# Transposing two units' activations by DMA instead of on TensorE, with half-width tiles at the start of a layer

## The chip, the cores and the metric

One core of one Trainium2 chip. The metric is the time of one execution in device microseconds; below, "time" is the median of the fast runs. Profiles come from the hardware profiler, one execution each. TensorE is PE, VectorE DVE, ScalarE ACT, GpSimd POOL, SyncE SP. SP and POOL issue the DMAs (and ACT the last store). The granted clock is TensorE's, as a share of its full speed.

## The reference, cut to what matters

Chunked attention is followed by a two-layer feed-forward block:

```python
scores = scale * q_c @ k_c.T             # 8 batches x 8 heads, chunks of 64 tokens, head size 64
attn   = exp(scores) / sum               # in each chunk
x      = (attn @ v_c) as (4608 tokens, 512)
h      = x @ w_in                        # 512 -> 2048
g      = h * 1 / (1 + exp(-beta * h))
out    = g @ w_out                       # 2048 -> 512
```

## The kernel before

The 4608 tokens are 18 units of 256; two units form a block of 512 (units 4 and 5 are block 2). The attention of later units is woven between the matmuls of earlier blocks. A unit has two halves `s` of 128 tokens. For each half, `emit_norm` (DVE) divides the weighted sum by its denominator and gives x in fp16. It has to be transposed before the first layer, on PE or by DMA:

```python
def emit_xt_pe(u, s, copy=nc.scalar.copy):
    xf = x16_t.pop((u, s)).rearrange("p r h d -> p (r h d)")
    ...                                                     # a PSUM bank for xp
    for g in range(4):
        nc.tensor.transpose(out=xp[:, g, :], in_=xf[:, g * 128:(g + 1) * 128], identity=ident)
    copy(out=xt_at(u, s), in_=xp)                           # on ACT

def emit_xt_dma(u, s):
    xf = x16_t.pop((u, s)).rearrange("p r h d -> p (r h d)")
    nc.sync.dma_start_transpose(out=xt_at(u, s), in_=xf)    # on SP's queue
```

Before the change, units 0 to 5 go by PE and units 6 to 17 by DMA. One first-layer tile, and where its result goes:

```python
def emit_m(j, m, c0=0, n=None, later=False):    # tile m of block j; n columns from c0, all 512 by default
    hps = ps_p.tile([128, 512], FP32, tag="p", name="hps")   # one of four PSUM banks, shared with ops
    for kk in range(4):
        nc.tensor.matmul(out=hps[:, 0:n], lhsT=w_in..., rhs=xt..., ...)
    sg = ...                                                 # ACT: tanh(beta/2 * hps)
    ...                                                      # DVE: gt = (sg + 1) * hps; then the bank is free
```

`emit_t(j, t, k0, k1)` are the second layer's matmuls of output tile t (`ops`), `emit_sc`/`emit_pv` a unit's scores and weighted sum, `emit_T` transposes q and k. `loads_to(u)` puts a unit's loads of q, k and v (six for unit 9) on POOL's DMA queue. They convert fp32 to fp16 and write 128-byte rows.

The softmax here doesn't subtract the row's maximum and nothing guards it: scores larger than these inputs give would overflow.

Of the kernel before, what the change touches and what calls it, by code (L numbers as in the profile page):

```python
# [15 lines left out]
def kernel(  # L16
# [16 lines left out]
    KFF = DFF // 128  # L33
# [91 lines left out]
    def loads_to(u):  # L125
        while nxt[0] <= min(u, NU - 1):
            load_unit(nxt[0])
            nxt[0] += 1
# [16 lines left out]
    def emit_T(u, which=("kT", "qT")):  # L145
        for nm in which:
            src, dst = {"kT": (k_t, kT), "qT": (q_t, qT)}[nm]
            a = src.pop(u)
            t = qt_p.tile([128, H, CH, 2], FP16, tag=nm, name=nm)
            dst[u] = t  # L150
            if u >= XU:
                nc.sync.dma_start_transpose(
                    out=t.rearrange("p h s e -> p (h s e)").rearrange("p (j t) -> p j t", t=128),
                    in_=a.rearrange("p h r d -> p (h r d)"),
                )
                continue
            nc.vector.transpose(
                out=t.rearrange("p h s e -> p (h s e)").bitcast(FP32).rearrange(
                    "p (h i r) -> p h r i", h=H, r=2),
                in_=a.rearrange("p h r d -> p (h r d)").bitcast(FP32).rearrange(  # L160
                    "p (h r i) -> p h r i", h=H, r=2),
            )
        if which[-1] == "qT" and u not in (6, 7, 8):
            loads_to(u + 4)

    def emit_gate(u):
        nc.gpsimd.tensor_copy(out=gate, in_=x16_t[u, 1][:, 0, 0, 0:1])
# [86 lines left out]
    def emit_pv(u, where=("x", "s")):  # L254
        et = et_t.pop(u)
        for s in (1, 0) if u >= MU else (0, 1):
            i = 2 * u + s
            if where[s] == "p":
                x = [ps_p.tile([128, 4, 128], FP32, tag="p", name=f"y{r}") for r in range(2)]
            else:  # L260
                pool = {"x": ps_x, "s": ps_s}[where[s]]
                x = [pool.tile([128, 2, 4, 128], FP32, tag=where[s], name="x")]
            for g in range(4):
                for r in range(2):
                    for c in range(2):
                        nc.tensor.matmul(  # L266
                            out=(x[0][64 * c:64 * c + 64, r, g, 0:D + 1] if len(x) == 1 else
                                 x[r][64 * c:64 * c + 64, g, 0:D + 1]),
                            lhsT=(et[64 * r:64 * r + 64, s, 4 * c + g, :] if u < XU else
                                  et[64 * r:64 * r + 64, g % 2, 4 * s + 2 * c + g // 2, :]),  # L270
                            rhs=vbig[64 * r:64 * r + 64, i, 4 * c + g, 0:D + 1],
                        )
            x_t[u, s] = x
# [6 lines left out]
    def emit_norm(u, s):  # L280
        x = x_t.pop((u, s))
        rd = rd_p.tile([128, 2, 4, 1], FP32, tag="rd", name="rd")
        x16 = x_p.tile([128, 2, 4, D], FP16, tag="x16", name="x16")
        for r, z in [(slice(0, 2), x[0])] if len(x) == 1 else list(enumerate(x)):
            nc.vector.reciprocal(out=rd[:, r], in_=z[..., D:D + 1])  # L285
            o = x16[:, r]
            nc.vector.tensor_tensor(  # L287
                out=o, in0=z[..., 0:D], in1=rd[:, r].to_broadcast(list(o.shape)), op=ALU.mult
            )
        x16_t[u, s] = x16  # L290

    def xt_at(u, s):
        j, o = unit_block[u]
        if j not in xt_t:
            xt_t[j] = xt_p.tile([128, 4, 4, 128], FP16, tag="xt", name="xt")
        return xt_t[j][:, 2 * o + s]

    def emit_xt_pe(u, s, copy=nc.scalar.copy):
        xf = x16_t.pop((u, s)).rearrange("p r h d -> p (r h d)")
        tag = "s" if u < 2 and (u, s) != (1, 0) else "xp"[s]  # L300
        xp = {"x": ps_x, "s": ps_s, "p": ps_p}[tag].tile([128, 4, 128], FP16, tag=tag, name="xp")
        for g in range(4):
            nc.tensor.transpose(out=xp[:, g, :], in_=xf[:, g * 128:(g + 1) * 128], identity=ident)  # L303
        copy(out=xt_at(u, s), in_=xp)  # L304
# [11 lines left out]
    def emit_xt_dma(u, s):  # L316
        xf = x16_t.pop((u, s)).rearrange("p r h d -> p (r h d)")
        nc.sync.dma_start_transpose(out=xt_at(u, s), in_=xf)
# [3 lines left out]
    def emit_m(j, m, c0=0, n=None, later=False):  # L322
        n = blocks[j][1] * UNIT if n is None else n
        if j not in gt_t:
            gt_t[j] = gt_p.tile([128, KFF, 512], FP16, tag="gt", name="gt")
        hps = ps_p.tile([128, 512], FP32, tag="p", name="hps")
        xr = xt_t[j].rearrange("p t (r k) (c q) -> p (t r) (k c) q", r=2, c=2)
        for kk in range(KDM):
            nc.tensor.matmul(  # L329
                out=hps[:, 0:n],  # L330
                lhsT=w_in16[m // 2][:, kk, (m % 2) * 128:(m % 2) * 128 + 128],
                rhs=xr[:, c0 // CH:(c0 + n) // CH, 2 * (kk % 2) + kk // 2, :],
                start=(kk == 0),
                stop=(kk == KDM - 1),
            )
        sg = sg_p.tile([128, 512], FP32, tag="sg", name="sg")

        def act():
            nc.scalar.activation(  # L339
                out=sg[:, 0:n], in_=hps[:, 0:n], func=ACTF.Tanh, scale=beta2[:, m:m + 1])  # L340

        def vec():
            nc.vector.scalar_tensor_tensor(  # L343
                out=gt_t[j][:, m, c0:c0 + n], in0=sg[:, 0:n], scalar=1.0, in1=hps[:, 0:n],
                op0=ALU.add, op1=ALU.mult,
            )

        if later:
            return act, vec
        act()  # L350
        vec()
# [3 lines left out]
    def emit_t(j, t, k0=0, k1=None):  # L355
        k1 = KFF if k1 is None else k1
        if k0 == 0:
            ops_t[j, t] = ps_p.tile([128, DM], FP32, tag="p", name="ops")
        ops = ops_t[j, t]
        for kk in range(k0, k1):  # L360
            nc.tensor.matmul(  # L361
                out=ops,
                lhsT=gt_t[j][:, kk, t * 128:(t + 1) * 128],
                rhs=w_out16[kk // 4][:, kk % 4, :],
                start=(kk == 0),
                stop=(kk == KFF - 1),
            )
        if k1 < KFF:
            return
        osb = osb_p.tile([128, DM], FP32, tag="osb", name="osb")  # L370
        nc.scalar.activation(out=osb, in_=ops, func=ACTF.Copy, scale=0.5)  # L371
        r0 = blocks[j][0] * UNIT + t * 128
        nc.sync.dma_start(out=out[r0:r0 + 128, :], in_=osb)
# [20 lines left out]
    with tc.manual_schedule():  # L394
# [111 lines left out]
                emit_ex(4)  # L506
        emit_t(1, 0, 0, 8)
        emit_pv(4)
        emit_norm(4, 0)
        emit_norm(4, 1)  # L510
        emit_T(5)
        emit_T(6)
        emit_t(1, 0, 8)
        emit_xt_pe(4, 0)
        emit_xt_pe(4, 1)
        emit_t(1, 1, 0, 8)
        emit_sc(5)
        emit_t(1, 1, 8)
        emit_pv(5)
        emit_norm(5, 0)  # L520
        emit_norm(5, 1)
        emit_T(7)
        emit_t(1, 2, 0, 8)
        emit_xt_pe(5, 0)
        emit_xt_pe(5, 1)
        emit_sc(6)
        emit_t(1, 2, 8)
        for m in range(KFF):
            emit_m(2, m)
            if m == 0:  # L530
                emit_pv(6)
                emit_norm(6, 0)
                emit_xt_dma(6, 0)
            if m == 1:
                emit_norm(6, 1)
                emit_gate(6)
                emit_xt_dma(6, 1)
                loads_to(10)
                emit_t(1, 3, 0, 8)
                emit_T(8)  # L540
            if m == 4:
                emit_sc(7)
            if m == 5:
                emit_t(1, 3, 8)
            if m == 7:
                emit_pv(7)
                emit_norm(7, 0)
                emit_xt_dma(7, 0)
            if m == 8:
                emit_norm(7, 1)  # L550
                emit_gate(7)
                emit_xt_dma(7, 1)
                loads_to(11)
# [90 lines left out]
```

## Time and profile before

| | |
|---|---|
| time, 3 runs | 288.05 us (287.95 to 288.5) |
| profiled span, granted PE clock | 286.6 us, 0.999 |
| PE busy | 280.4 us |
| PE waits on a DMA | none |

The prediction shows the page's main lines, and lines of the timeline (start in us, duration, instruction, count). This is PE's timeline where block 3 starts (start in us, duration, instruction, count), then the view of the last transpose of x that this block needs, issued at 91.24 us:

```profile
94.71 1.89 PE L361 MATMUL ops<-wout,gt 128*128 128x512 f16 x8
96.44 0.81 PE L329 MATMUL hps<-xt,win 128*128 128x512 f16 x3
```
```profile
DMA to landing us min/median/max: 4.1/4.1/4.1
```

The transpose lands at 95.3 us and PE wants it at 96.44: 1.1 us to spare, which no list of waits shows. At block 5 it is 1.3 us (154.24 against 155.54).

### The profile page before, as it was taken

What the parts mean: (1) busy time and instruction counts of PE and PEld (TensorE: products, weight loads), DVE (VectorE), ACT (ScalarE), POOL (GpSimd) and SP (SyncE); (2) the same over time, 40 slices, a digit from 0 to 9 for tenths busy, and PEclk for the clock granted to TensorE, in tenths of its full rate; (3) what the DMA queues carried; (4) which work ended last, traced back from release to release, by engine and by line L of the source; (5) the groups of instructions that cost most, each with busy time, mean ns of one, the idle gap of its engine ahead of it and who ended that gap; (6) DMA issues with size and microseconds to landing.
All of it is one profiled execution on the core that took longest, in us unless ns stands there. A gap on an engine that the chain in (4) does not pass through costs nothing.

```text
span 286.6 us, 6655 instructions
## 1 busy us (share of the span) xinstructions
PE 280.4 (98%) x2777; PEld 136.4 (48%) x2777; DVE 141.9 (49%) x260; ACT 147.0 (51%) x225; POOL 95.7 (33%) x125
## 2 busy tenths in 40 slices
PE   6989999999999999999999999999999999999995
PEld 3564456545544444444444444444444444444444
DVE  2778444776567544534454445454554545333300
ACT  3478228774557545454545454554545444444411
POOL 8853678487172992070907160000000000000000
PEclk9999999999999999999999999999999999999999
DMA  8999999999999999999999999565451212010012
GB/s 193 175 196 206 182 180 215 206 166 165 153 95 182 155 176 167 165 119 168 137 158 145 143 124 171 129 75 128 57 129 39 73 39 73 37 39 37 37 73 75
DMA packets 139997, 37.14 MB, mean 130 GB/s; under 512 B 126912, under 2 KB 135488, under 8 KB 139968
## 3 DMA queue, kind: packets, MB, share of 16 engines
q0 software_dynamic: 99136, 17.83, 82.4%
q1 hardware_dynamic: 40688, 18.83, 32.2%
q8 instruction: 22, 0.36, 0.5%
q14 instruction: 7, 0.06, 0.1%
q10 hardware_dynamic: 144, 0.07, 0.1%
HBM read 36.71 MB, written 9.44 MB: 161 GB/s over the span
## 4 chain that ended last, share of the span: by engine, by line
PE 96%; ACT 1%; POOL 1%; issue 1%; DVE 0%; DVEq 0%; POOLq 0%
PE hps L329 44%; PE ops L361 43%; PE warm L381 2%; PE x L266 2%; PE sc L238 1%; PE sc L225 1%; PE ops L600 1%; ACT xt L304 1%; PE xp L303 1%; POOL h L401 1%; PE sc L198 1%; POOL vbig L113 1%; ACT et L208 0%; PE y L266 0%; PE xp L311 0%
## 5 line engine op out<-in xcount | busy, mean ns | idle before, releaser
L343 DVE SCALAR_TENSOR_TENSOR gt<-sg,hps 128x512 f16<-128x512 f32 (+1 forms) x153 | 99.1, 654 | 107.4 <-ACT sg L339 107.2
L339 ACT ACTIVATE sg<-hps,beta 128x512 f32<-128x512 f32 (+1 forms) x153 | 100.4, 663 | 72.9 <-PE hps L329 72.8
L329 PE MATMUL hps<-xt,win 128*128 128x512 f16 (+1 forms) x612 | 136.8, 367 | 0.8 <-ACT xt L304 0.7
L361 PE MATMUL ops<-wout,gt 128*128 128x512 f16 x560 | 131.2, 379 | 0.0
L329 PEld LDWEIGHTS <-win 128*128 128x128 f16 x612 | 58.1, 98 | 62.1 <-issue 1.0
L361 PEld LDWEIGHTS <-gt 128*128 128x128 f16 x560 | 53.9, 98 | 63.4
L371 ACT ACTIVATE osb<-ops 128x512 f32<-128x512 f32 x35 | 20.9, 598 | 42.5 <-PE ops L361 42.5
L113 POOL DMA_DIRECT2D vbig<-in_v_dram x40 | 34.1, 871 | 9.6 <-DMA wout<-in_moe_w_out_dram 3.7
L99 POOL DMA_DIRECT2D qu<-in_q_dram x22 | 18.7, 863 | 40.1 <-DMA qT<-qu 37.1
L287 DVE TENSOR_TENSOR x<-x,rd 128x512 f16<-128x512 f32 x31 | 21.4, 691 | 1.2
L99 POOL DMA_DIRECT2D ku<-in_k_dram x22 | 18.9, 877 | 0.6 <-DMA ku<-in_k_dram 0.6
L285 DVE RECIPROCAL rd<-x 128x8 f32<-128x8 f32 x31 | 6.2, 200 | 12.0 <-PE x L266 12.0
L247 ACT ACTIVATE et<-sc 128x1024 f16<-128x1024 f32 (+1 forms) x8 | 6.4, 811 | 8.2 <-PE sc L238 8.2
L231 ACT ACTIVATE et<-sc 128x1024 f16<-128x1024 f32 x10 | 10.2, 1018 | 0.2
L266 PEld LDWEIGHTS <-et 64*64 64x64 f16 x576 | 6.0, 107 | 7.3 <-issue 3.8
L381 PE MATMUL warm<-idle 128*128 128x512 f16 x22 | 8.2, 518 | 0.0
L105 POOL DMA_DIRECT2D ku<-in_k_dram x9 | 6.8, 756 | 2.5 <-DMA win<-in_moe_w_in_dram 1.3
L266 PE MATMUL x<-vbig,et 64*64 64x65 f16 x496 | 7.3, 194 | 0.2 <-ACT et L208 0.2
L105 POOL DMA_DIRECT2D qu<-in_q_dram x9 | 6.8, 767 | 1.4 <-DMA win<-in_moe_w_in_dram 0.7
L612 DVE TENSOR_SCALAR osb<-ops 128x256 f32<-128x256 f32 (+1 forms) x2 | 0.7, 357 | 12.1 <-PE ops L600 12.1
L131 POOL DMA_DIRECT2D win<-in_moe_w_in_dram x8 | 6.0, 757 | 1.2 <-DMA vbig<-in_v_dram 0.9
L304 ACT COPY xt<-xp 128x512 f16<-128x512 f16 x9 | 5.1, 588 | 2.3 <-PE xp L303 2.2
(46 smaller groups left out, 73.4 us busy)
## 6 DMA issues: line engine op xcount, KB each, us to landing
out_dram<-osb SPq DMA_DIRECT2D x35, 256.0 KB, 3.7
vbig<-in_v_dram POOLq DMA_DIRECT2D x32, 128.0 KB, 7.6
qu<-in_q_dram POOLq DMA_DIRECT2D x20, 128.0 KB, 4.9
ku<-in_k_dram POOLq DMA_DIRECT2D x20, 128.0 KB, 6.8
win<-in_moe_w_in_dram POOLq DMA_DIRECT2D x8, 256.0 KB, 9.0
wout<-in_moe_w_out_dram POOLq DMA_DIRECT2D x4, 512.0 KB, 12.3
qu<-in_q_dram POOLq DMA_DIRECT2D x3, 256.0 KB, 7.7
ku<-in_k_dram POOLq DMA_DIRECT2D x3, 256.0 KB, 8.0
```

The costliest lines, as they stand in the source:

```text
L99: nc.gpsimd.dma_start(out=tv[off:off + n, sp], in_=src[b, :, s:s + n, :].rearrange("h p d -> p h d"),)
L105: nc.gpsimd.dma_start(out=t[off // 2:(off + n) // 2], in_=src[b, :, s:s + n, :].rearrange("h (p r) d -> p h r d", r=2),)
L113: nc.gpsimd.dma_start(out=vbig[off:off + n, i, :, 0:D], in_=v[b, :, s:s + n, :].rearrange("h p d -> p h d"),)
L231: nc.scalar.activation(out=et, in_=sc, func=ACTF.Exp, scale=scale)
L266: nc.tensor.matmul(out=(x[0][64 * c:64 * c + 64, r, g, 0:D + 1] if len(x) == 1 else x[r][64 * c:64 * c + 64, g, 0:D + 1]), lhsT=(et[64 * r ...
L287: nc.vector.tensor_tensor(out=o, in0=z[..., 0:D], in1=rd[:, r].to_broadcast(list(o.shape)), op=ALU.mult)
L329: nc.tensor.matmul(out=hps[:, 0:n], lhsT=w_in16[m // 2][:, kk, (m % 2) * 128:(m % 2) * 128 + 128], rhs=xr[:, c0 // CH:(c0 + n) // CH, 2 * ...
L339: nc.scalar.activation(out=sg[:, 0:n], in_=hps[:, 0:n], func=ACTF.Tanh, scale=beta2[:, m:m + 1])
L343: nc.vector.scalar_tensor_tensor(out=gt_t[j][:, m, c0:c0 + n], in0=sg[:, 0:n], scalar=1.0, in1=hps[:, 0:n], op0=ALU.add, op1=ALU.mult,)
L361: nc.tensor.matmul(out=ops, lhsT=gt_t[j][:, kk, t * 128:(t + 1) * 128], rhs=w_out16[kk // 4][:, kk % 4, :], start=(kk == 0), stop=(kk == K ...
L371: nc.scalar.activation(out=osb, in_=ops, func=ACTF.Copy, scale=0.5)
L381: nc.tensor.matmul(out=d[:, 0:w], lhsT=idle[:, 0:128], rhs=idle[:, 0:w])
```

## The change

The intent: take 16 transposes off the engine that sets the time, and hide the DMA's latency by starting block 2's first layer with tiles that need unit 4 only.

```diff
         emit_pv(4)
+        emit_norm(4, 1)
+        emit_xt_dma(4, 1)
+        emit_T(5)
         emit_norm(4, 0)
-        emit_norm(4, 1)
-        emit_T(5)
+        emit_xt_dma(4, 0)
         emit_T(6)
         emit_t(1, 0, 8)
-        emit_xt_pe(4, 0)
-        emit_xt_pe(4, 1)
...
         emit_norm(5, 0)
+        emit_xt_dma(5, 0)
         emit_norm(5, 1)
+        emit_xt_dma(5, 1)
         emit_T(7)
         emit_t(1, 2, 0, 8)
-        emit_xt_pe(5, 0)
-        emit_xt_pe(5, 1)
         emit_sc(6)
         emit_t(1, 2, 8)
-        for m in range(KFF):
-            emit_m(2, m)
+        order = [(m, 0, 256) for m in range(6)]
+        for m in range(6, KFF):
+            order.append((m, 0, None))
+            if m < 12:
+                order.append((m - 6, 256, 256))
+        done = 0
+        for m, c0, n in order:
+            emit_m(2, m, c0, n)
+            done += 1 if n else 2
...      # the other work hangs on the same places: unit 6 after half tiles 1 and 3, emit_sc(7) after the first full
...      # tile, emit_t(1, 3, 8) after half (0, 256), emit_pv(7) and emit_norm(7, ..) after halves (2, 256), (3, 256)
```

More of the change, by code (lines that the diff above doesn't have):

```diff
@@ L520 @@
         emit_norm(5, 0)
+        emit_xt_dma(5, 0)
         emit_norm(5, 1)
+        emit_xt_dma(5, 1)
         emit_T(7)
         emit_t(1, 2, 0, 8)
-        emit_xt_pe(5, 0)
-        emit_xt_pe(5, 1)
         emit_sc(6)
         emit_t(1, 2, 8)
-        for m in range(KFF):
-            emit_m(2, m)
-            if m == 0:
+        order = [(m, 0, 256) for m in range(6)]
[7 more added lines that the diff above has]
+            done += 1 if n else 2
+            if done == 2:
                 emit_pv(6)
@@ L533 @@
                 emit_xt_dma(6, 0)
-            if m == 1:
+            if done == 4:
                 emit_norm(6, 1)
@@ L540 @@
                 emit_T(8)
-            if m == 4:
+            if (m, n) == (6, None):
                 emit_sc(7)
-            if m == 5:
+            if (m, c0, n) == (0, 256, 256):
                 emit_t(1, 3, 8)
-            if m == 7:
+            if (m, c0, n) == (2, 256, 256):
                 emit_pv(7)
@@ L548 @@
                 emit_xt_dma(7, 0)
-            if m == 8:
+            if (m, c0, n) == (3, 256, 256):
                 emit_norm(7, 1)
```

## The prediction

> **What bounds the kernel now.** I read the page's first two parts, then the chain of work that ended last, the chain between 62 and 76 us (where the four transposes of x stand), and the busy time by stretch.
>
> ```profile
> span 286.6 us, 6655 instructions
> PE 280.4 (98%) x2777; PEld 136.4 (48%) x2777; DVE 141.9 (49%) x260; ACT 147.0 (51%) x225; POOL 95.7 (33%) x125
> ...
> PE 96%; ACT 1%; POOL 1%; issue 1%; DVE 0%; DVEq 0%; POOLq 0%
> ```
> ```profile
> 66.12 0.45 PE xp L303 x8
> 66.57 1.73 PE ops L361 x8
> 68.30 0.64 PE sc L238 x64
> 68.94 1.83 PE ops L361 x8
> 70.77 0.38 PE x L266 x32
> 71.14 1.83 PE ops L361 x8
> 72.98 0.45 PE xp L303 x8
> 73.42 0.64 PE sc L238 x64
> ```
> ```profile
> 62.00:76.00 14.00, 14.00 (x259) 7.36 (x258) 7.72 (x16) 6.43 (x11) 9.24 (x11) 1.00 2.11 168
> 76.00:96.00 20.00, 20.00 (x214) 9.30 (x213) 13.45 (x24) 13.04 (x19) 9.83 (x14) 1.00 1.34 140
> 96.00:260.00 164.00, 164.00 (x1359) 75.55 (x1358) 77.35 (x136) 83.58 (x122) 35.60 (x43) 1.00 1.03 113
> ```
>
> The page says that TensorE is busy for 98% of the span and carries 96% of the chain. The chain lines show eight `xp` transposes of unit 4 in 0.45 us and eight of unit 5 in another 0.45 us, in the middle of a stream without a hole. The stretches (columns: us, then busy us of PE, PEld, DVE, ACT and POOL, then granted clock, DMA share, GB/s) show PE without a gap from 62 to 260 us at full clock. So the time is the sum of what TensorE is given: an instruction taken from it shortens the run by its own spacing, unless TensorE then waits for something.
>
> **What the Trainium skill says.** "TensorE: Matmul & The Clock Gate", section "Back-to-back issue gap", gives N/2.4 + 2.5 ns between isolated warm matmuls of N columns, and for sustained streams 81 ns at N=128 and 131 ns at N=512. This trace follows the first formula: eight 512-column matmuls take 1.73 us (216 ns each), eight 128-column transposes 0.45 us (56 ns each). I use these. The same page, "Part 4: PE-mode transpose", puts a transpose at about 275 ns in a kernel. The instruction table here has a duration of 219 ns, but that is latency: the spacing of 56 ns is what the stream pays, so counting 16 durations would overstate the gain fourfold. "DMA: Bandwidth & Descriptors", section "Issuing engines are not separate DMA queues", says that DMAs from different engines run on the same 16 DMA engines and interleave. The trace agrees: the same xt transpose landed 2.5 us after issue at 79.1 us, where the loads were quiet (DMA share 0.29 in 78 to 82), and 7.2 us after issue at 105.1 us, beside loads (share 2.27 in 102 to 108). "Perfetto Trace Analysis", section "Identifying the Most-Contended Engine", warns that matmul busy share is no measure of roofline headroom; I use it only to say that no gap is left.
>
> **The change part by part.** Removed: 16 transposes from TensorE, 0.45 + 0.45 = 0.90 us of the path by the chain's lines, 0.89 by 16 x 55.8 ns. Four ScalarE copies of about 0.59 us go too. ScalarE is busy 6.43 of the 14 us there and TensorE waited for none of them, so they weren't on the path.
>
> Added to TensorE: six tiles of four 512-column matmuls become twelve of four 256-column ones. Widths from the block before, which has both:
>
> ```profile
> 46.11 0.61 PE L329 MATMUL hps<-xt,win 128*128 128x256 f16 x4
> 46.56 1.03 PE L361 MATMUL ops<-wout,gt 128*128 128x512 f16 x4
> 47.42 0.39 PE L303 MATMUL xp<-ident,x 128*128 128x128 f16 x4
> 47.65 0.60 PE L329 MATMUL hps<-xt,win 128*128 128x256 f16 x4
> ```
>
> In the last line four start within 0.60 minus one latency of 0.27, so 0.109 us apart; a half tile is 0.437 us, a full one 0.863 (4 x 0.216). Splitting a tile costs 0.011 us, six cost 0.07. Weight loads (98 ns) still fit under 109 ns.
>
> Moved: unit 4's x now goes out by DMA. From the order of instructions, unit 4's second half is normalized first, at about 65.3 us, and its first half at about 67.4 us (after unit 5's q and k transposes). The first half-width tile needs both and comes at 75.73 - 0.89 = 74.84 us. That leaves 7.4 us for the later one, just more than the worst xt landing, 7.2 us. Unit 5's halves are issued at about 71.6 and 72.9 us, since one issue takes the queue 1.2 us. The first full tile needs them after six half tiles (2.62 us), the weighted sum of unit 6 (0.47 with its change of shape) and eight output matmuls (1.73): 4.82 us on, at 79.66 us. That is 6.8 us after the later issue; the median landing of the 24 xt transposes is 2.9 us (list of DMA issues). The six half tiles exist to buy these 4.8 us. I expect no wait on either.
>
> Added behind TensorE: VectorE. In the run of tiles at the end of this layer it is already late in the kernel before:
>
> ```profile
> 88.24 0.69 DVE L343 SCALAR_TENSOR_TENSOR gt<-sg,hps 128x512 f16<-128x512 f32 x1 [0.17 <-ACT sg L339]
> 88.85 0.20 DVE L285 RECIPROCAL rd<-x 128x8 f32<-128x8 f32 x1
> 89.08 0.69 DVE L287 TENSOR_TENSOR x<-x,rd 128x512 f16<-128x512 f32 x1
> 89.69 0.68 DVE L343 SCALAR_TENSOR_TENSOR gt<-sg,hps 128x512 f16<-128x512 f32 x1
> 90.28 0.20 DVE L285 RECIPROCAL rd<-x 128x8 f32<-128x8 f32 x1
> 90.52 0.69 DVE L287 TENSOR_TENSOR x<-x,rd 128x512 f16<-128x512 f32 x1
> ```
>
> Spacings: a full gate product 0.60 us, a normalization 0.84. The pairs of the block before (x2 groups of 1.02 us, second duration 0.41) give 0.33 us behind a half product. In before, a tile arrives each 0.86 us, so VectorE gains 0.26 us a tile. In after, a full and a half tile arrive each 1.30 us and cost 0.93, and unit 7's two normalizations (1.68 us) fall among them.
>
> Step by step from 0 at the first half tile: on TensorE tile 8 starts at 9.90, its second-half partner (tile 2) at 10.76, tile 9 at 11.67 (after unit 7's weighted sum), then 12.54, tile 10 at 12.97, 13.84, tile 11 at 14.27, 15.14, tile 12 at 15.57. ScalarE can start a full tile 1.065 us after TensorE does, and VectorE 0.72 after that, so tile 8's product starts at 11.69 and tile 2's at 12.29. Then: normalization at 12.62, tile 9 at 13.46, tile 3's half at 14.06, second normalization at 14.39, tile 10 at 15.23. This ends at 15.92. By the pool's four banks, as the built program assigns them, tile 12 is written into tile 10's bank: TensorE wants it at 15.57 and gets it at about 15.95. That is a wait of 0.38 us, the one I expect. Tile 11 (bank free at about 14.18, wanted at 14.27) just passes, and after tile 12 VectorE catches up.
>
> The scores of unit 6 wait for the second normalization of unit 5, which ends at about 72.40 us against 72.46 wanted: a few hundredths at most.
>
> Sum: -0.89 + 0.07 + 0.38 = -0.44 us, so 288.05 - 0.44 = 287.6 us.
>
> **The rivals.** First: no bank wait. If VectorE is 0.4 us earlier than I reckon, the whole -0.82 stays: 287.2 us. For it: in before, the wait list of TensorE names no VectorE wait here, although the backlog there reached four products back to back. Against: the before has no half tiles among its normalizations. Second: a DMA wait takes the transposes' place. Unit 4's later transpose is issued at about 67.4 us among loads (DMA share 2.03 in 66 to 72), and a landing after 7.4 us would stop TensorE before its first half tile. For it: 7.2 us was seen at share 2.27. Against: the store issued at 66.8 us landed in 3.7 us. Another 1 us of delay costs nearly 1 us, so 288.0 to 289.5 us. Third: ScalarE becomes the bound on the half tiles, since 0.48 us of duration exceeds TensorE's 0.437. Against: in the pairs of the block before two activations take 1.05 us against 1.30 of TensorE, and the weighted sum and eight output matmuls interrupt the six. I give it nothing.
>
> **Range and chances.** Most likely some of the bank wait (0.2 to 0.6 us), so 287.4 to 287.8. About one in five that it is absent (287.2), about one in eight that a DMA lands late (288 or more). Runs of the same kernel spread over 0.55 us (287.95 to 288.5). So 287.0 to 288.3 should hold it 8 times in 10. None of the cases reaches 2% (5.8 us): within 2% 0.985, faster 0.005, slower 0.01.
>
> **What would show it.** Right: no PE transposes after the first two blocks; unit 6's scores start about 0.9 us earlier than 73.35 us; four 256-column matmuls per 0.44 us; xt transposes of unit 4 landed before the first half tile; one PE gap of about 0.4 us late in this layer, released by VectorE's gate product. Wrong: a PE wait on an xt transpose before the first half or first full tile (late landing), a gap after it elsewhere, or no gap and a full 0.8 us gain. I'd be wrong altogether if the earlier loads and transposes upset the later DMA traffic and PE gaps appear after 96 us.

## The result, and the profile after

The changed kernel takes 289.64 us (289.53 to 290.23, 6 runs) against 288.36 us of before (287.95 to 289.33, 6 runs, which include the three above): ratio 1.0045, 95% interval 1.0027 to 1.0063. A ratio is the mean time of one kernel's fast runs over that of the other's of the same rounds, so not quite the ratio of the medians quoted.

So it is 1.3 us slower, where 0.44 us faster was foreseen. That is under half a per cent, but the interval lies above 1. From the page of the changed kernel:

```profile
span 287.8 us, 6697 instructions
PE 90%; DMA 3%; DVE 2%; ACT 1%; POOL 1%; issue 1%; DVEq 0%; POOLq 0%
```

A DMA is on the chain now, with 3% of the span. The piece of the chain that is it (start, us, what):

```profile
73.30 7.60 DMA xt<-x
80.89 0.14 issue
81.03 1.02 PE hps L329 x4
```

The last transpose of unit 5 is issued at 73.30 and lands 7.60 us later; the first full-width tile starts right behind it. PE's timeline (in brackets: idle before, and what ended it):

```profile
72.76 0.71 PE L238 MATMUL sc<-qT,kT 32*64 32x64 f16 x64
75.14 1.04 PE L329 MATMUL hps<-xt,win 128*128 128x256 f16 x8
79.10 1.04 PE L329 MATMUL hps<-xt,win 128*128 128x256 f16 x8
81.03 1.02 PE L329 MATMUL hps<-xt,win 128*128 128x512 f16 x4 [0.90 <-DMA xt<-x]
92.21 3.61 PE L329 MATMUL hps<-xt,win 128*128 128x512 f16 x16 [0.23 <-DVE gt L343]
```

Unit 6's scores start at 72.76 us, before 73.35: the gain of the removed transposes is there (0.59 us, and this run's first layer had begun 0.30 us later). The half tiles start without a wait at 75.14, so unit 4's transposes are in time. Then the two gaps. The brackets count idle from the modelled end of the matmul before. What the stream loses is the spacing of starts beyond the usual one: at 81.03 it is 1.17 - 0.11 = 1.06 us, at 92.21 it is 0.50 - 0.11 = 0.39 us.

DVE ahead of the second gap, in the order that the prediction reckoned (two products, a normalization, two products, a normalization):

```profile
88.86 0.20 DVE L285 RECIPROCAL rd<-x 128x8 f32<-128x8 f32 x1
89.09 0.69 DVE L287 TENSOR_TENSOR x<-x,rd 128x512 f16<-128x512 f32 x1
89.70 1.02 DVE L343 SCALAR_TENSOR_TENSOR gt<-sg,hps 128x512 f16<-128x512 f32 x2
90.64 0.20 DVE L285 RECIPROCAL rd<-x 128x8 f32<-128x8 f32 x1
90.87 0.69 DVE L287 TENSOR_TENSOR x<-x,rd 128x512 f16<-128x512 f32 x1
91.48 1.61 DVE L343 SCALAR_TENSOR_TENSOR gt<-sg,hps 128x512 f16<-128x512 f32 x3
```

Tile 10's product starts at 91.48 without a pause behind the normalization, and the bank is free 0.7 us later: at 92.2, when tile 12 starts.

**A measure without the start-up.** The first first-layer matmul starts anywhere from 14.80 to 16.62 us in the 14 profiles, whatever the kernel, so spans mix in noise larger than the effect. I compare the PE stream: from the start of the first first-layer matmul to the start of the last output matmul. Before: 283.45 - 15.28 = 268.17 us. After: 284.40 - 15.58 = 268.82, that is +0.65. The parts: -0.89 (transposes) + 0.07 (splits) + 1.06 + 0.39 = +0.63 us.

**Behind the last matmul** the changed kernel is slower once more: 3.41 us to the end of the span in place of 3.16. SP ends with nine waits in a row for DMA semaphores, in a fixed order and 0.06 us apart. The store that lands last (2.24 us after the last matmul starts, in both) is the last of these waits in before, while in the changed kernel four more waits follow it. I take it that the four added DMAs on SP's queue shift which semaphore tells of which store; this is read from the traces and wasn't tried by itself. All nine other profiles with both units' transposes by DMA have a tail of 3.40 or 3.41 us too; the split-only run, which keeps them on PE, has 3.16. With two DMAs added (e4 below) six waits follow the last landing, and the tail is 3.53 us. Only e10's 3.31 us has another reason: its last store lands 2.39 us after the last matmul starts, not 2.24.

### The profile page after: what moved, and what is told of

It reads as the page before. It is cut to its first block, busy times and chain, and to the rows that moved or that the text cites. A ratio compares the mean times of both kernels' runs of the same rounds, so it can differ in the third digit from the quotient of the medians.

```text
span 287.8 us, 6697 instructions
## 1 busy us (share of the span) xinstructions
PE 280.2 (97%) x2785; PEld 137.7 (48%) x2785; DVE 142.3 (49%) x266; ACT 145.9 (51%) x227; POOL 95.7 (33%) x125
## 4 chain that ended last, share of the span: by engine, by line
PE 90%; DMA 3%; DVE 2%; ACT 1%; POOL 1%; issue 1%; DVEq 0%; POOLq 0%
PE hps L329 41%; PE ops L361 40%; DMA xt<-x 3%; PE warm L381 2%; PE x L266 2%; PE sc L225 1%; PE ops L607 1%; PE sc L238 1%; DVE x L287 1%; ACT xt L304 1%; DVE gt L343 1%; POOL h L401 1%; PE sc L198 1%; POOL vbig L113 1%; ACT et L208 0%
## 5 line engine op out<-in xcount | busy, mean ns | idle before, releaser
L329 PE MATMUL hps<-xt,win 128*128 128x512 f16 (+1 forms) x636 | 137.2, 359 | 2.0 <-DMA xt<-x 0.9
L329 PEld LDWEIGHTS <-win 128*128 128x128 f16 x636 | 60.3, 98 | 62.2 <-issue 1.4
L179 DVE STREAM_TRANSPOSE t<-h 128x512 f32<-128x512 f32 (+1 forms) x5 | 4.1, 900 | 3.3 <-ACT h L178 3.3
```

The lines of the kernel that those rows point to most:

```text
L329: nc.tensor.matmul(out=hps[:, 0:n], lhsT=w_in16[m // 2][:, kk, (m % 2) * 128:(m % 2) * 128 + 128], rhs=xr[:, c0 // CH:(c0 + n) // CH, 2 * ...
```

## The experiments

My theory after the result: unit 5's transposes wait behind the loads of unit 9. Those are issued by POOL from 67 us on, beside them. From the trace, packets started in half a microsecond (a load's packet is 128 bytes, one of an x transpose 256):

```
changed kernel      76.0   76.5   77.0   77.5
loads                538    491    188     82
stores                 8      4      0      0
x transposes           0     47    254    138
```

The first transpose of unit 5 was issued at 71.89 us; its first packet starts at 76.6 us, when the loads begin to thin out. It isn't only the loads that go first: two stores stand ahead of it on SP's own queue, issued at 69.22 and 71.28 us, and their 256 packets start between 72.51 and 76.83 us. They are slow too: from 74.0 to 74.5 us 610 load packets start and none of theirs. Rival theories: the transposes and stores ahead on SP's own queue would delay it without the loads too; or the half tiles themselves cost time.

Each group of runs had its own runs of before on the same chip: 288.64, 288.38 and 288.68 us (11 runs each). "Stream" is the PE stream of the one profiled run against before's 268.17 us. Before was profiled only once; e10, which is before with fewer loads, has the same stream to 0.01 us.

| run | time, us (range) | ratio, 95% interval | stream |
|---|---|---|---|
| e1 split only | 288.84 (288.48 to 289.01) | 1.0005, 0.9992 to 1.0018 | +0.45 |
| e2 no split | 296.37 (295.70 to 296.87) | 1.0267, 1.0248 to 1.0285 | +8.12 |
| e3 late loads | 292.16 (290.70 to 294.40) | 1.0129, 1.0087 to 1.0171 | +3.90 |
| e4 unit 4 only | 289.82 (288.92 to 290.46) | 1.0040, 1.0021 to 1.0059 | +0.58 |
| e5 the change again | 290.83 (289.56 to 292.38) | 1.0084, 1.0060 to 1.0109 | +2.09 |
| e6 unit 7 earlier | 289.91 (289.26 to 291.95) | 1.0059, 1.0034 to 1.0085 | +0.78 |
| e7 full tiles later | 289.49 (288.47 to 290.27) | 1.0034, 1.0017 to 1.0052 | +0.09 |
| e8 both | 289.42 (287.98 to 291.81) | 1.0031, 0.9994 to 1.0068 | +0.98 |
| e9 change, fewer loads | 288.36 (287.80 to 288.77) | 0.9990, 0.9977 to 1.0003 | -0.44 |
| e10 before, fewer loads | 288.27 (288.06 to 288.61) | 0.9990, 0.9978 to 1.0002 | 0.00 |
| e11 both, fewer loads | 287.89 (287.48 to 288.46) | 0.9975, 0.9962 to 0.9987 | -0.74 |
| e12 both, halves in blocks 3 to 5 | 288.04 (287.75 to 288.54) | 0.9983, 0.9971 to 0.9995 | -0.51 |

The first and third group ran on one chip, the second (e5 to e8) on another. Each kernel has six runs, e10 and e12 five, e2 four. Only e2 differs from before by more than 2%.

### e1: the split alone

The attention part as in before, the first layer in the changed order.

```diff
-        emit_norm(4, 1); emit_xt_dma(4, 1); emit_T(5); emit_norm(4, 0); emit_xt_dma(4, 0)
+        emit_norm(4, 0); emit_norm(4, 1); emit_T(5); ... emit_xt_pe(4, 0); emit_xt_pe(4, 1)
...                                                       # unit 5 likewise
```

> Transposes of x of units 4 and 5 stay on the PE, only the six half-width tiles of unit 4 come first. My accounting (split costs 0.07 us, VectorE backlog makes tile 12 wait 0.3 to 0.4 us for its PSUM bank, the DMA landing is the rest): +0.4 to +0.5 us against before, no PE wait on a DMA, one PE gap of about 0.3 us released by the gate product. Rival (the split itself is what costs, by ScalarE or VectorE on the half tiles): +1.3 us or more, with gaps on the half tiles. Rival (bank wait is a consequence of the late DMA): the gap is absent and the time is +0.1 us.

```profile
91.59 1.67 PE L329 MATMUL hps<-xt,win 128*128 128x512 f16 x7 [0.23 <-DVE gt L343]
```

PE has this one gap and no wait on a DMA; the stream is +0.45 us. The bank wait exists without any late DMA, with the size reckoned, and the half tiles cost nothing else. The timed difference, +0.05%, is less than that, but its interval (-0.2 to +0.5 us) holds it.

### e2: the DMA transposes alone

```diff
-        order = [(m, 0, 256) for m in range(6)] ...
+        for m in range(KFF):
+            emit_m(2, m)                       # and the rest of the loop as in before
```

> Transposes by DMA as in the change, but full-width tiles in the order of before, so the first tile needs unit 5 at once. If the landing of unit 5's x is what sets the wait: PE stops before the first tile for about 5.5 us (landing at 80 to 81 us, wanted at 75), no bank wait, time +4 to +5 us against before. If landings follow what TensorE does (they come earlier when less is issued): a wait of under 3 us and +2 us or less.

```profile
80.83 1.44 PE L329 MATMUL hps<-xt,win 128*128 128x512 f16 x3 [6.07 <-DMA xt<-x]
```

The transpose is issued at 72.72 us and lands at 80.70, after 8.0 us; in the change, where PE worked on, it took 7.6. So a standing PE doesn't bring the landing forward. The loss is larger than I expected (+7.7 us in time and +8.1 in the stream, in place of +4 to +5): after the stop PE runs at half its clock for 6 us. The line has the stretch, its length, the busy us of PE, PEld, DVE, ACT and POOL, then clock, DMA share and GB/s:

```profile
80.80:86.80 6.00, 5.97 (x45) 2.30 (x46) 2.40 (x6) 1.38 (x2) 0.00 (x0) 0.50 0.10 22
```

The granted clock is 0.50 in this stretch, and a 512-column matmul takes 0.427 us in place of 0.216. The Trainium skill, "TensorE: Matmul & The Clock Gate", section "Why this matters for your kernels", warns of PE idle gaps of more than about 3 us for this reason, and this run agrees. The gap of about 1 us in the change did no such harm. The six half tiles thus are worth far more than the wait they shorten.

### e3: unit 9's loads later

```diff
-        if which[-1] == "qT" and u not in (6, 7, 8):
+        if which[-1] == "qT" and u not in (5, 6, 7, 8):
             loads_to(u + 4)
...
             emit_m(2, m, c0, n)
+            if (m, c0) == (0, 0):              # the copy makes POOL wait for the first gate product
+                nc.gpsimd.tensor_copy(out=gate, in_=gt_t[2][:, 0, 0:1])
+                loads_to(9)
```

> The change, but the loads of unit 9 wait for the first half tile's gate product (about 76 us) in place of starting at 67 us. If the xt transposes of unit 5 are late because they queue behind these loads on the 16 DMA engines: they land about 3 us after issue (by 77 us), the PE wait before the first full tile is gone, the bank wait of 0.2 to 0.4 us stays, time -0.2 to -0.6 us against before. If they are late because of the transposes and stores ahead of them on their own queue: landing still at 79 to 81 us, wait 0.5 us or more, time as the change.

The landing is as the theory has it: unit 5's last transpose, issued at 72.79, lands in 3.3 us, at 76.08.

```profile
DMA to landing us min/median/max: 3.3/3.3/3.3
```

The two stores stand ahead of unit 5's transposes here too (issued at 68.54 and 70.90), but without loads beside them their packets have all started by 72.5 us, and the first transpose's follow at 72.7. So the stores and transposes ahead on the queue don't make it late without the loads. What the stores add beside the loads wasn't tried by itself.

PE's timeline has no gap there, but a new one where block 3 starts (and one of 2.24 us at block 5):

```profile
78.71 1.90 PE L329 MATMUL hps<-xt,win 128*128 128x256 f16 x12
...
97.95 0.38 PE L329 MATMUL hps<-xt,win 128*128 128x512 f16 x1 [1.88 <-DMA xt<-x]
```

The time I missed, by far: +3.7 us in place of -0.2 to -0.6. The loads now run while unit 7's transposes want the DMA engines. The last of them takes 7.7 us to land (4.1 before) and is 2 us late, and unit 11's is late too. The loads that held up one transpose were moved onto others.

### e4: unit 4 only by DMA

```diff
         emit_norm(5, 0)
-        emit_xt_dma(5, 0)
         emit_norm(5, 1)
-        emit_xt_dma(5, 1)
         emit_T(7)
         emit_t(1, 2, 0, 8)
+        emit_xt_pe(5, 0)
+        emit_xt_pe(5, 1)
```

> Unit 4's x by DMA, unit 5's by PE, half-width tiles as in the change. By my accounting: -0.45 (8 transposes) +0.07 +0.3 to 0.4 (bank wait), no DMA wait: -0.1 to +0.1 us against before. If unit 4's landing too is on the edge: a PE gap before the first half tile and +0.3 us or more.

There is no wait on unit 4 (landed at 73.35 us) and the bank wait is 0.39 us, as expected. But block 5's first tile starts 0.58 us late, 0.09 us after unit 11's last transpose has landed at 155.93 us (154.24 in before). -0.44 + 0.07 + 0.39 + 0.58 = +0.60, and the stream shows +0.58. My expectation of about zero missed this: the loss lies 75 us later than the change. How the change reaches that far wasn't traced, and the profile itself puts this wait down to "issue", not to a DMA: that it is the transpose is read from the two times. The tail takes another 0.37 us.

### e5: the change again

> The change itself, run again as the control of this group and for a second profile. +1.0 to +1.6 us against before; a PE wait of 0.5 to 1.5 us before the first full tile (unit 5's landing at 80.5 to 81.5 us) and one of 0.3 us at tile 12. If waits on xt appear at the first tiles of blocks 3 or 5 as well, they account for what the first profile of the change (0.65 us by its PE stream) lacked against the timed runs (1.3 us).

```profile
82.74 0.59 PE L329 MATMUL hps<-xt,win 128*128 128x512 f16 x2 [1.57 <-DMA xt<-x]
```
```profile
158.97 0.38 PE L329 MATMUL hps<-xt,win 128*128 128x512 f16 x1 [0.63 <-DMA xt<-x]
```

In this execution unit 5's transpose took 8.2 us, the wait cost the stream 1.74 us, and the first tile of block 5 lost 0.80 us: -0.82 + 1.74 + 0.39 + 0.80 = +2.11 (stream +2.09). So the waits on DMA differ from run to run, and a single profile of the change showed a mild case. This one shows a bad case: the profiled run took 292.38 us, the slowest of its six, though 1.34 us of that is a later start of the first layer. In this group the change was 2.4 us slower than before, above the 1.0 to 1.6 expected; in the first comparison it was 1.3. Why the groups differ I leave open.

### e6: unit 7's normalizations earlier

```diff
             if (m, c0, n) == (0, 256, 256):
                 emit_t(1, 3, 8)
-            if (m, c0, n) == (2, 256, 256):
                 emit_pv(7); emit_norm(7, 0); emit_xt_dma(7, 0)
-            if (m, c0, n) == (3, 256, 256):
-                emit_norm(7, 1); emit_gate(7); emit_xt_dma(7, 1)
+                emit_norm(7, 1); emit_xt_dma(7, 1)
+            if (m, c0, n) == (3, 256, 256):
+                nc.gpsimd.tensor_copy(out=gate, in_=gt_t[2][:, 3, 256:257])
                 loads_to(11)
```

> The change, with unit 7's weighted sum and both normalizations moved ahead of tile 7, where VectorE is idle (loads of unit 11 keep their time by a gate on a gate product). If the wait at tile 12 comes from the normalizations among the half tiles: that PE gap (0.39 us) is gone, the wait on unit 5's x stays at 0.5 us or more; 0.3 to 0.5 us less than the change. If the half tiles alone overload VectorE: the gap stays.

```profile
84.93 7.32 PE L329 MATMUL hps<-xt,win 128*128 128x512 f16 x43
```

43 matmuls without a break up to the window's end, where the change had its gap at tile 12: it was DVE's normalizations among the half tiles, not the half tiles. The wait on unit 5 remains (1.49 us of the stream). The median is 0.9 us below the change's of the same group, but with the spread of both (2.7 and 2.8 us) the intervals overlap, so the times don't settle even the direction; the removed gap is read from the stream.

### e7: the first full tile later

```diff
-            if (m, n) == (6, None):
+            if (m, c0) == (5, 0):
                 emit_sc(7)
-            if (m, c0, n) == (0, 256, 256):
                 emit_t(1, 3, 8)
```

> The change, with unit 7's scores and the second half of the last output tile put ahead of the first full tile, which so is wanted 2.4 us later (about 82.5 us). If unit 5's landing is fixed by the DMA traffic (80 to 81 us whatever the PE does, as in the run without half tiles): the PE wait before the first full tile is gone, about 0.9 us less than the change. If the landing moves with what the PE does: a wait of 0.5 us or more stays.

The profile lists no PE wait on a DMA; the first full tile starts at 83.11 us. Unit 5's first half lands at 80.79 us, as in the change (80.61); the landing of the second isn't in this trace. The bank wait remains (0.39 us), and 0.45 us is lost within unit 7's scores. The stream is +0.09 us, where the change had +2.09 in its run of this group (e5), and the time is 1.3 us below the change's. So the landing doesn't move with what PE does, which is what the traffic theory has it do. By its ratio the time is still 1.0 us above before.

### e8: both

The edits of e6 and e7 together.

> Both of these. By my sum -0.89 + 0.07 and neither wait: -0.8 us against before (287.4 to 288.0). Rival: DMA traffic up to 185 us is a second bound, so that a PE which runs 0.8 us earlier waits for xt at the first tile of block 3 or 5, where the kernel before has only 1.1 and 1.3 us to spare: then -0.4 to +0.3 us, with those waits in the profile.

```profile
97.61 0.59 PE L329 MATMUL hps<-xt,win 128*128 128x512 f16 x2 [1.36 <-DMA xt<-x]
```

The rival was right about the place, but not about the size (+0.9 us by the ratio, where it had +0.3 at most) nor wholly about the way. Block 2 has no wait any more, and the wait has gone to block 3 (1.53 us of the stream, and 0.28 at block 5). It isn't only that PE comes earlier: unit 7's last transpose was issued 3 us earlier than in before (88.23 against 91.24), and landed 2 us later (97.47 against 95.32). Single runs reach 287.98 us, others 291.81.

### e9, e10, e11: fewer loads

If loads are the cause, taking some away must give the predicted sum. From unit 9 on, k isn't loaded and q stands in for it. The arithmetic is wrong (the scores are so small that the result still passed the comparison). All other instructions stay. e9 is the change, e10 before, e11 the version of e8.

```diff
         for src, dst, nm in ((q, q_t, "qu"), (k, k_t, "ku")):
+            if u >= 9 and nm == "ku":
+                dst[u] = q_t[u]
+                continue
```

> The change, with k of units 9 to 17 not loaded (q stands in for it, so the result is wrong on purpose; every other instruction stays). If the loads are what holds up the xt transposes: unit 5's last half lands 1.5 us or more earlier (by 79.5 us for a start of unit 5's issue at 72 to 73), the PE wait before the first full tile falls to 0.3 us or less, the waits on xt in blocks 3 and 5 are gone; the bank wait of 0.3 us stays, so -0.5 to -0.2 us against before. If the transposes and stores on their own queue are the cause: landing and waits as in the change, +0.7 us or more.

> The same lighter loads in the kernel before: control. Its PE stream has no wait on a DMA in the profile, so -0.3 to +0.1 us against before; if it gains more than 0.5 us, the kernel before already loses time to xt in its unprofiled runs.

> The lighter loads in the version with both waits reordered away: if the loads are the second bound, the full sum of -0.8 us against the lighter before (-0.7 to -1.1 us against before), a narrow spread, no PE wait on xt. If not: waits at the first tile of block 3 or 5 as in the version with full loads.

In e9, unit 5's last transpose lands at 78.47 us, 5.9 us after its issue, and PE waits for no DMA anywhere. Its list of waits has, behind the start-up, only the bank wait (three lines were added, so L332 is L329 elsewhere):

```profile
DMA to landing us min/median/max: 5.9/5.9/5.9
```
```profile
PE hps L332 <- DVE gt L346: 0.2, 1, 0.2
```

The stream is -0.44 us: the sum, to the hundredth. e11, without the bank wait, is at -0.74 and 0.25% (0.7 us) faster than before; against the lighter before, where I expected -0.8 us, the ratios give only -0.4, and these two intervals overlap. e10 shows that before itself has little to gain from fewer loads: its stream is unchanged, -0.1% in time with an interval that holds zero. In time e9 is level with e10: its tail is 0.10 us longer than e10's (3.41 against 3.31), and the 0.34 us left of the 0.44 are below what these runs resolve (each interval is nearly 0.4 us to either side). So the sum is shown in the stream, not in the time.

### e12: a correct version with all loads

e8, and in blocks 3, 4 and 5 the first two tiles are split as well, so that the second unit's x is wanted later there:

```diff
-                if it[0] == "m":
+                if it[0] == "m" and j < 6 and it[1] < 2:
+                    emit_m(j, it[1], 0, 256)
+                elif it[0] == "m":
                     emit_m(j, it[1])
+                    if j < 6 and it[1] < 4:
+                        emit_m(j, it[1] - 2, 256, 256)
```

> Correct version, all loads: both waits reordered away as above, and in blocks 3, 4 and 5 the first two tiles are split as well, so that the second unit's x is wanted some 3.5 us later. If the remaining loss of that version is only the wait on unit 7's and unit 11's x: -0.6 to -0.9 us against before (287.5 to 287.8), no PE wait on xt in the profile. If the delay simply moves on to the next need: a PE wait of 0.5 us or more at another DMA (q and k transposes, or the third tile of those blocks).

PE waits for no DMA in the profile though unit 7's last transpose took 7.8 us. With 288.04 us and a ratio of 0.9983 (interval below 1) this beats before by a little and the change, each set against the before of its own group, by well over 1 us; its runs lie within 0.8 us. Its gain of 0.5 us is a bit short of the 0.6 to 0.9 expected. The stream is -0.51: the six further splits cost 0.07, and 0.23 us is lost within unit 7's scores, as in e7. The tail takes 0.24 of it.

## Why the prediction was wrong

- **The bound, and what the transposes cost.** Right. The stream gains 0.89 us, six splits cost 0.07: e9 has this sum and the bank wait, -0.44 us, with nothing left over.
- **The bank wait at tile 12.** Right in place, cause and size: 0.38 foreseen, 0.39 measured (also in e1, without any DMA). e6 shows the cause.
- **Unit 4's landing.** Right: landed at 73.2 us, wanted at 75.14.
- **Unit 5's landing: the step that failed.** It reads "That is 6.8 us after the later issue; the median landing of the 24 xt transposes is 2.9 us (list of DMA issues)", and then "I expect no wait on either." The landing took 7.60 us (8.2 in e5), the issue came at 73.3 in place of 72.9. For unit 4 I had compared the slack with the worst landing, 7.2 us, but for unit 5 with the median of 24 transposes, ten of them from the quiet part after 175 us, where they take 2.4 or 2.5 us. The loads of unit 9 were in flight in both cases, and two stores stood ahead on the queue. With 7.2 us in this place too (72.9 + 7.2 = 80.1 against 79.66 wanted), a wait of 0.4 us would have been on the table. The cause is shown by e3 (loads moved: 3.3 us), e9 (a third of them taken away: no wait) and e2 (PE stopped: same landing).
- **The second rival** had the mechanism, a DMA wait in place of the transposes, but was put on unit 4 and given one chance in eight. Its form, another 1 us of delay costs nearly 1 us, holds.
- **What none of the steps had.** "PE gaps appear after 96 us" was named only as a sign of being wrong altogether. Before has no such gaps, but only 1.1 and 1.3 us to spare at blocks 3 and 5. In e3, e4, e5 and e8 that was used up, in the first profile of the change it wasn't. And 0.24 us of tail that no one would look for.

Together: -0.82 + 0.39 + 1.06 to 1.74 (unit 5) + 0 to 0.80 (block 5) + 0.24 (tail) = +0.9 to +2.4 us from two profiled runs, against +1.3 and +2.4 for the medians of their groups. (That the upper ends agree is partly luck: e5's profile is of its slowest run.) That is where the expected gain went: into transfers that share the DMA engines with the loads.

What stays open: why the loads leave the packets of the stores and transposes waiting as long as they do (the queues don't seem to share evenly: 610 packets against none in the half microsecond named above), how much of the landing time the two stores ahead account for, and whether a 16 KB packet of the instruction queue, which takes 1.7 us at 77 us in the change, adds to it.

## What to carry to other kernels

Moving work from a saturated engine to the DMA engines exchanges a known cost for a landing time: compare the slack with the landings of the same transfer beside the same traffic, never with the median over the run, and count what stands ahead on its own queue. An engine without waits can have slack of a microsecond at several places that no list shows; measure issue, landing and first use for each before shifting traffic. If a transfer can't be made earlier, start its consumer with the part that doesn't need it, at each place where the slack is thin, and keep other engines' work out of the stretch where the pieces are smaller.

## What the Trainium skill lacked or had wrong

- "TensorE: Matmul & The Clock Gate", "Back-to-back issue gap": the sustained spacings of 81 ns (128 columns) and 131 ns (512) don't hold here. The stream has 56, 109 and 216 ns for 128, 256 and 512 columns, as the page's formula for isolated matmuls gives.
- The same page, "Part 4: PE-mode transpose": about 275 ns per transpose in a kernel. Here 219 ns of duration, and 56 ns of the stream in a row of them; the page gives no spacing for transposes.
- "DMA: Bandwidth & Descriptors", "Latency and other measured facts", gives about 600 ns to the first byte of such a DMA. A transpose at 79.11 us with quiet loads had its first packet 1.3 us after the start of its issue; the one at 71.89 us, beside loads and behind two stores of its own queue, 4.7 us after it. No page gives a figure for a transfer beside a burst of small-packet loads from another queue, which was the whole question here.
- No page has the spread of the start-up: the first first-layer matmul came at 14.80 to 16.62 us over 14 profiles, more than the effect studied.
- No page has the waits at the end of a kernel: SP's waits of 0.06 us each in a fixed order, of which none, four or six follow the last landing (3.16, 3.41 or 3.53 us of tail).
